# The last tile's third part in its own piece of PSUM, its first part's residual and store a tile earlier, and three stores right behind their residuals

## The chip, the cores and the metric

The kernel runs on one core of a Trainium2 chip. The metric is the device time of one execution in microseconds. The core's engines work side by side, each through its own queue in order: TensorE (PE in the profile; its weight loads are PEld), VectorE (DVE), ScalarE (ACT), GpSimd (POOL) and SyncE (SP), which here issues the transfers between the core and its memory. An engine waits for another one by semaphores.

## The reference

Two blocks stand one behind the other, on 2048 rows of 640 columns, in bfloat16:

```python
x = A_q
h = x + _A_ref(_layernorm(x, axis=-1), A_k, A_v, A_shift_k, A_ssm_k, A_ssm_D)
h2 = h + _B_ref(_layernorm(h, axis=-1), B_w1, B_b1, B_w2)
return h2
```

`_A_ref` is a short convolution of `k`, a product with `v`, a long convolution over all rows, and a product with the normalized input. The change doesn't touch it. `_B_ref` is a dense layer of two matrices with Mish in between:

```python
h = jnp.einsum("bsd,df->bsf", x, w1) + b1
sp = jnp.log1p(jnp.exp(-jnp.abs(h))) + jnp.where(h > 0, h, jnp.zeros_like(h))
act = h * jnp.tanh(sp)
return jnp.einsum("bsf,fd->bsd", act, w2)
```

The sum of `h` and the result of `_B_ref` is the output. The change lies in this sum and in the product with `w2` ahead of it.

## The kernel before

**Tiles.** The 2048 rows are 16 tiles of 128 rows. A tile's `h` lies in one of three buffers of the on-chip memory: `x0` (tiles 0 to 3; `x` in the profile), `xa` (4 to 9) and `xb` (10 to 15). For the dense layer the tiles are taken in five units of 2, 2, 4, 4 and 4 tiles. For a unit, the normalized rows are transposed: by TensorE for the first three units, and for tiles 8 to 15 by VectorE (`dtr8` and so on, line 788) and then by 16 small transfers for each pair of tiles (`d_tr8`, `d_tr10`, `d_tr12`, `d_tr14`, line 804). Then come seven steps `m1pe<unit>_<n>` of the first product (lines 845 and 849), each followed by Mish on ScalarE (`hb<unit>_<n>`, line 858).

**The second product.** For tile t, `m2pe<t>` is 28 matmuls (line 875): for each half of 320 columns, 14 matmuls of 128 rows by 320 columns, which add up in PSUM. When they are done, `res<t>` on VectorE (line 885) adds the PSUM result to the tile's rows in place, and `d_out<t>` on SP (line 890) stores the 160 KB.

**The last tile** is cut into three parts by columns, `TAIL`: 320, 224 and 96 of them. `m2ape15`, `m2bpe15` and `m2cpe15` are the matmuls of the three parts (14 each, line 875), `resa15`, `resb15` and `resc15` their residuals (line 882), `d_outa15`, `d_outb15` and `d_outc15` their stores (line 897). All three parts lie in one piece of PSUM. Part a takes columns 0 to 319 of the piece, part b columns 512 to 735 and part c columns 736 to 831.

**PSUM** is used as four pieces of 128 × 1024 float32 (`ps0` to `ps3`; `ps` in the profile), a ring named `R_PS`. A step that opens a result takes one, and the piece is free again when the last reader of that result is done. Where several are free, the planner takes the one that it expects to have come free first. The framework under the kernel sets the semaphores, from the order in which the instructions are written down and from the buffers that they touch.

**Order.** The order of all steps is written out by hand, as `ORDER`: a name and a letter for the engine (`t` TensorE, `a` ScalarE, `v` VectorE, `p` GpSimd, `d` the SP queue). On each engine the steps run in that order. `_schedule` gives each step a start by costs that the kernel holds, and the steps are written down in the order of these starts; so among engines it is these starts that decide which step is written down first. In the planner's times `resa15` starts when `res14` ends, which is after the start of `m2bpe15` and before that of `m2cpe15`.

In the order before, the last steps of TensorE are m2pe11, m1pe4_3, m2pe10, m2ape15, m2pe13, m2pe12, m2pe14, m2bpe15, m2cpe15; those of VectorE are res10, res13, res12, res14, resa15, resb15, resc15; and the stores on SP are d_out10, d_out13, d_out12, d_out14, d_out8, d_outb15, d_outa15, d_outc15. Earlier on SP, d_tr8 stands ahead of d_out1, d_out0 and d_tr10; d_out2 and d_out3 come behind d_tr10; d_out9 stands ahead of d_out4.

Of the kernel before, what the change touches and what calls it, by code (L numbers as in the profile page):

```python
# [27 lines left out]
TAIL = [(0, 320), (320, 224), (544, 96)]  # L28
# [31 lines left out]
hb0_2:a hb0_0:a m1pe0_1:t hb0_1:a m1pe0_3:t hb0_3:a wb6:v ln1_11:v trpe2:t pow3:p hc3:v m1pe0_5:t trev2:a hb0_5:a wb4:v wb5:v h5:p trpe3:t trev3:v  # L60
m1pe0_4:t h6:p ln1_14:v bn5:v wb7:v hb0_4:a ln1e3:p h4:v bn6:v bn4:v ln1p3:p m1pe1_2:t hb1_2:a pow5:p pow6:p m1pe1_3:t hb1_3:a lnx9:a pow4:p hc4:v
m1pe1_6:t hc6:v h7:v hc5:v m1pe1_1:t hb1_1:a m1pe1_0:t m1pe1_4:t hb1_6:a lnx8:a wb8:v h8:v lnx10:a hb1_0:a hb1_4:a m2pe1:t trpe4:t trpe6:t trev4:a
bn7:v pow7:p hc7:v trev6:a res1:v wb9:v h9:v bn9:v pow9:p m1pe1_5:t trpe5:t trpe7:t hb1_5:a bn8:v pow8:p hc8:v trev5:a hc9:v wb10:v dtr8:v dtr9:v
d_tr8:d d_out1:d m2pe0:t trev7:a m1pe2_6:t h10:p bn10:v pow10:p m1pe2_3:t hb2_3:a hb2_6:a res0:v d_out0:d hc10:v lnx11:a m1pe2_2:t ln1_12:v dtr10:v
ln1_15:v wb11:v ln1_13:v h11:v bn11:v pow11:p hb2_2:a hc11:v dtr11:v d_tr10:d ln1e4:v ln1p4:p lnx14:p m2pe2:t res2:v lnx13:p wb13:v i2pa14:t i2pb14:t
i2pa12:t i2pc14:t y14:a wb14:v i2pb12:t i2pc12:t y12:a m1pe2_1:t hb2_1:a m1pe2_5:t hb2_5:a i2pa15:t i2pb15:t i2pc15:t y15:v m1pe2_4:t hb2_4:a lnx15:a
d_out2:d h13:p lnx12:p wb12:p h12:p m1pe2_0:t m2pe3:t bn13:v pow13:p res3:v d_out3:d h14:v bn14:v pow14:p bn12:v pow12:p hc12:v dtr12:v hc13:v dtr13:v
hb2_0:a d_tr12:d m2pe5:t res5:v d_out5:d m2pe6:t res6:v d_out6:d m1pe3_2:t hb3_2:a wb15:v h15:p bn15:v pow15:p m2pe7:t res7:v d_out7:d hc14:v
m1pe3_1:t hb3_1:a m1pe3_0:t dtr14:v hb3_0:a hc15:v dtr15:v d_tr14:d m1pe3_4:t m1pe3_3:t hb3_3:a m1pe3_5:t hb3_5:a hb3_4:a m1pe3_6:t hb3_6:a m2pe4:t
res4:v m2pe9:t res9:v d_out9:d d_out4:d m2pe8:t res8:v m1pe4_1:t m1pe4_6:t hb4_6:a m1pe4_5:t hb4_5:a hb4_1:a m1pe4_4:t m1pe4_2:t hb4_2:a m1pe4_0:t  # L70
hb4_0:a m2pe11:t res11:v d_out11:d m1pe4_3:t hb4_3:a m2pe10:t res10:v d_out10:d hb4_4:a m2ape15:t m2pe13:t res13:v d_out13:d m2pe12:t res12:v
d_out12:d m2pe14:t res14:v d_out14:d resa15:v d_out8:d m2bpe15:t resb15:v d_outb15:d d_outa15:d m2cpe15:t resc15:v d_outc15:d
""".split()
UNITS = [256, 256, 512, 512, 512]

# [112 lines left out]
def _dve1(n):  # L188
    return 0.06 + 0.001045 * n
# [14 lines left out]
def _mm(n):  # L204
    return max(0.027, n / 2400.0 + 0.0025)
# [46 lines left out]
def kernel(  # L252
# [18 lines left out]
    def OP(name, opts, deps=(), allocs=(), uses=(), emit=None, prio=0.0, lat=0.0):  # L271
        o = _Op(name, opts if isinstance(opts, list) else [opts], deps, allocs, uses, emit, prio, lat)
        ops.append(o)
        return o
# [56 lines left out]
    for c in CHUNKS:  # L331
# [4 lines left out]
        for x in SWT[c.i]:  # L336
            t = blk(x)
# [16 lines left out]
    R_PS = _Ring(4)  # L354
# [12 lines left out]
    def ps_f32(rt):  # L367
        rt.tile = banks[rt.slot][:]
        return rt.tile
# [125 lines left out]
    for b in range(NDC):  # L495
        rt = _RT(R_PS)
# [17 lines left out]
    for m in range(NDC):  # L514
        for h in (1, 0):
            rt = _RT(R_PS)
# [13 lines left out]
            def kvf(e, m=m, h=h, rt=rt):  # L530
# [3 lines left out]
                             uses=[rt], emit=kvf, prio=9.2))  # L534
# [4 lines left out]
    for b in range(NDC):  # L539
        n = raw_n[b]  # L540
        rt = _RT(R_PS)
# [29 lines left out]
    for gi in range(22):  # L571
        rt = _RT(R_PS)
# [30 lines left out]
    for c in CHUNKS:  # L603
        nf = (32, 16, 8)[len(c.dcs) - 1]
        n = c.ng
        evs = []
        for gi in range(P // nf):
            rt = _RT(R_PS)
# [49 lines left out]
    for c in CHUNKS:  # L658
        for gi in range(c.ng // 8):
            rt = _RT(R_PS)  # L660
# [25 lines left out]
    w2_z = OP("w2z", ("pool", 1.25), k1_pes + d_adds, emit=emit_w2z, prio=7)  # L686
    d_w2 = DMA("d_w2", 2.2e6, emit_w2, deps=i1_pes[1] + d_w1, prio=7)
# [29 lines left out]
    for t2 in range(NT):  # L717
# [10 lines left out]
        rt = _RT(R_PS)  # L728
# [97 lines left out]
    def hb_of(u):  # L826
        return hb_s[u % 2]
# [4 lines left out]
    for u, w in enumerate(UNITS):  # L832
        t2s = list(range(c0 // P, (c0 + w) // P))
        hbs = []
        for fp in range(NFC // 2):
            rt = _RT(R_PS)

            def pe(e, u=u, fp=fp, rt=rt, w=w):
                ph = ps_f32(rt)
                for i in range(2):  # L840
                    fc = fp * 2 + i
                    if fc == NFC - 1:
                        for dc in range(NDC):
                            for o in (0, 64):
                                nc.tensor.matmul(ph[o:o + 64, 512:512 + w // 2], w1[:, dc, fc * P:FF], lnhT_of(u).rearrange("p t r c j -> p c (t r) j")[:, dc, o * w // 4096:(o + 64) * w // 4096],
                                                 start=(dc == 0), stop=(dc == NDC - 1))
                        continue
                    for dc in range(NDC):
                        nc.tensor.matmul(ph[:, i * 512:i * 512 + w], w1[:, dc, fc * P:fc * P + P], lnhT_of(u).rearrange("p t r c j -> p c (t r) j")[:, dc, 0:w // 32],  # L849
                                         start=(dc == 0), stop=(dc == NDC - 1))  # L850
            o_pe = OP(f"m1pe{u}_{fp}", ("pe", 10 * _mm(w) if fp < NFC // 2 - 1 else 7.5 * _mm(w) + 2 * _SWITCH), [tr_evs[t] for t in t2s] + d_w1 + mm2_last.get(u - 2, []), allocs=[rt],
                      uses=[lt_rts[u]], emit=pe, prio=100 + u)

            def hbf(e, u=u, fp=fp, rt=rt, w=w):
                for i in range(2):
                    fc = fp * 2 + i
                    n = w // 2 if fc == NFC - 1 else w
                    nc.scalar.activation(hb_of(u)[:, fc, 0:n], rt.tile[:, i * 512:i * 512 + n], ACT.Mish, bias=b1s[:, fc:fc + 1], scale=1.0)  # L858
            hbs.append(OP(f"hb{u}_{fp}", ("act", (2 if fp < NFC // 2 - 1 else 1.5) * _act(w) + 0.18), [o_pe, c_b1] + i1_pes[(1, 2)[u % 2]], uses=[rt], emit=hbf, prio=100 + u))
        lasts = []  # L860
        for tl, t2 in enumerate(t2s):
            rt = _RT(R_PS)

            def pe2(e, u=u, tl=tl, rt=rt, w=w, cols=((0, 320), (320, 320))):
                po = ps_f32(rt) if cols[0][0] == 0 else rt.tile
                for a, n in cols:
                    for fc in range(NFC):
                        o = tl * P
                        if w == P and fc == NFC - 1:
                            for h in range(2):  # L870
                                nc.tensor.matmul(po[64 * h:64 * h + 64, a + a // 320 * 192:a + a // 320 * 192 + n], hb_of(u)[:, fc, 0:64], w2[:, fc + h, a:a + n],
                                                 start=False, stop=True)
                            continue
                        x = 1 if fc == NFC - 1 and o >= w // 2 else 0
                        nc.tensor.matmul(po[:, a + a // 320 * 192:a + a // 320 * 192 + n], hb_of(u)[:, fc, o - x * w // 2:o - x * w // 2 + P], w2[:, fc + x, a:a + n],  # L875
                                         start=(fc == 0), stop=(fc == NFC - 1))

            def resf(e, t2=t2, rt=rt, part=None):
                if part:
                    a, n = part  # L880
                    x = xt(t2)[:, a:a + n]
                    nc.vector.tensor_tensor(x, rt.tile[:, a + a // 320 * 192:a + a // 320 * 192 + n], x, ALU.add)  # L882
                    return
                x = xt(t2).rearrange("p (a d) -> p a d", a=2)
                nc.vector.tensor_tensor(x, rt.tile[:].rearrange("p (a d) -> p a d", a=2)[:, :, 0:320], x, ALU.add)  # L885
            if t2 < NT - 1:
                o_pe2 = OP(f"m2pe{t2}", ("pe", 3.81), hbs + [d_w2, w2_z], allocs=[rt], emit=pe2, prio=100 + u + 0.5)
                lasts.append(o_pe2)
                o_res = OP(f"res{t2}", ("dve", _dve1(640)), [o_pe2], uses=[rt], emit=resf, prio=44)
                DMA(f"d_out{t2}", 164e3, (lambda t2=t2: nc.sync.dma_start(oview[:, t2, :], xt(t2))), deps=[o_res], prio=100 + u + 0.5)  # L890
                continue
            o_pe2 = None
            for i, (a, n) in enumerate(TAIL):
                o_pe2 = OP(f"m2{'abc'[i]}pe{t2}", ("pe", 14 * _mm(n) + 0.005), hbs + [d_w2, w2_z, o_pe2], allocs=[] if i else [rt], uses=[rt] if i else [], emit=(lambda e, f=pe2, a=a, n=n: f(e, cols=((a, n),))), prio=100 + u + 0.5)
                lasts.append(o_pe2)
                o_res = OP(f"res{'abc'[i]}{t2}", ("dve", _dve1(n)), [o_pe2], uses=[rt], emit=(lambda e, f=resf, a=a, n=n: f(e, part=(a, n))), prio=44)
                DMA(f"d_out{'abc'[i]}{t2}", n * 256, (lambda t2=t2, a=a, n=n: nc.sync.dma_start(oview[:, t2, a:a + n], xt(t2)[:, a:a + n])), deps=[o_res], prio=100 + u + 0.5)
        mm2_last[u] = lasts
        c0 += w
# [42 lines left out]
```

## Time and profile before

| | us |
|---|---|
| median of 3 runs | 232.42 (230.9 to 233.92) |
| the profiled execution, whole | 232.92 |
| its span, from the first to the last instruction | 231.1 |
| PE busy in the span | 218.8 (95%) |
| DVE, ACT, POOL busy | 141.7, 133.2, 63.8 |
| mean granted TensorE clock | 0.985 of full speed |

In a row of the timeline stand the start in the span, the length, the engine, the line of the kernel, the operation, what it writes and reads with the shapes, the number of instructions, and in brackets the idle time of the engine ahead of it with what ended that. `SPq` is SP's queue; the length of a transfer there is the time that issuing it took, not the transfer's own. In a row of the groups by form stand the shape and number, then the busy time and the mean length of one in ns, then idle time. In a row of the transfers stand what is written and read, the number, the size of one and the median time from issue to landing. In a row of the chain stand start, length and what held up the end; `issue` is time in which nothing visible was waited for. In a row of the stretches stand, for each engine, busy time and number of instructions, then the granted TensorE clock, the share of the transfer engines in use and GB/s. `q8 instruction` is the queue through which TensorE's instructions come in: packets, MB, share.

### The profile page before, as it was taken

The page shows a single profiled execution, that of the slowest core. Times are in us where ns is not written, and L with a number is a line of the kernel's source. Part 1 is how long each engine was busy: PE and PEld are TensorE (multiplying, and loading weights), DVE is VectorE, ACT ScalarE, POOL GpSimd, SP SyncE. Part 2 cuts the span into 40 slices and gives each one's busy share as a digit, 9 for nine tenths or more (in the row PEclk, how much of TensorE's full clock was granted, in tenths as well). Part 3 has the DMA queues.
Part 4 walks back from the last instruction along what each step waited for, and adds up shares of the span by engine and source line. Part 5 has one row for each costly group of instructions (what it writes and reads, how often), then busy time and mean ns, then how long its engine had stood idle before and what let it go on. Part 6 is the DMA issues. An engine that isn't in the chain of part 4 may idle for free.

```text
span 231.1 us, 6512 instructions
## 1 busy us (share of the span) xinstructions
PE 218.8 (95%) x2809; PEld 168.5 (73%) x2809; DVE 141.7 (61%) x262; ACT 133.2 (58%) x183; POOL 63.8 (28%) x87
## 2 busy tenths in 40 slices
PE   7996999999959999999999999999999999999991
PEld 2995999999859899889877474676545764567771
DVE  0786798889999698998968984477710120011121
ACT  2586799989997999699675264501137004512000
POOL 0517066006820028744921305922000000000000
PEclk9999799999997999999999999999999999999999
DMA  7999990693990059940000012120131010000002
GB/s 219 376 419 409 417 383 18 187 271 109 257 278 6 3 197 407 385 154 0 3 0 3 12 32 77 32 80 14 32 107 32 21 57 0 0 33 28 28 31 85
DMA packets 24479, 30.05 MB, mean 130 GB/s; under 512 B 6529, under 2 KB 20866, under 8 KB 24066
## 3 DMA queue, kind: packets, MB, share of 16 engines
q1 hardware_dynamic: 24160, 29.48, 36.9%
q8 instruction: 22, 0.36, 0.6%
q10 hardware_dynamic: 194, 0.15, 0.2%
q14 instruction: 7, 0.06, 0.1%
q0 software_dynamic: 96, 0.00, 0.0%
HBM read 20.45 MB, written 2.62 MB: 100 GB/s over the span
## 4 chain that ended last, share of the span: by engine, by line
PE 81%; ACT 5%; DVE 4%; issue 4%; DVEq 0%; ACTq 0%
PE ps L875 26%; PE ps L849 25%; PE ps L667 4%; PE ps L666 4%; ACT uv L377 4%; PE ps L737 4%; PE ps L579 4%; PE ps L472 3%; PE ps L615 3%; PE ps L502 2%; ACT uk L377 2%; DVE uk L379 2%; PE ps L525 1%; DVE uv L379 1%; PE ps L473 1%
## 5 line engine op out<-in xcount | busy, mean ns | idle before, releaser
L858 ACT ACTIVATE uv<-ps,b1s 128x512 bf16<-128x512 f32 (+1 forms) x70 | 36.4, 591 | 56.1 <-PE ps L849 36.2
L875 PE MATMUL ps<-rn,uv 128*128 128x320 bf16 (+2 forms) x462 | 62.4, 295 | 0.6 <-DVE xb L882 0.6
L849 PE MATMUL ps<-G 128*128 128x512 bf16 (+1 forms) x325 | 58.8, 337 | 0.2 <-DVE G L379 0.2
L875 PEld LDWEIGHTS <-uv 128*128 128x128 bf16 x462 | 44.4, 98 | 18.1 <-issue 0.9
L377 ACT CAST uk<-ps 128x1024 bf16<-128x1024 f32 (+2 forms) x52 | 47.5, 1032 | 5.7 <-PE ps L473 3.5
L849 PEld LDWEIGHTS <-G 128*128 128x128 bf16 x325 | 31.2, 98 | 23.5 <-issue 0.7
L377 ACT CAST uv<-ps 128x1024 bf16<-128x1024 f32 x32 | 29.8, 1084 | 1.7 <-PE ps L615 1.7
L885 DVE TENSOR_TENSOR xb<-ps,xb 128x640 bf16<-128x640 f32 x5 | 4.1, 825 | 31.5 <-PE ps L875 31.5
L666 PE MATMUL ps<-a,uv 128*128 128x128 bf16 x160 | 19.6, 227 | 0.3 <-ACT uv L377 0.3
L666 PEld LDWEIGHTS <-uv 128*128 128x128 bf16 x160 | 18.4, 116 | 0.0
L885 DVE TENSOR_TENSOR xa<-ps,xa 128x640 bf16<-128x640 f32 x6 | 4.8, 814 | 20.4 <-PE ps L875 20.4
L768 POOL TENSOR_TENSOR r<-ve,mhalf 128x1 f32<-128x1 f32 x16 | 8.9, 561 | 24.1 <-DVE ve L765 24.1
L615 PE MATMUL ps<-uv,G 128*128 128x64 bf16 (+1 forms) x384 | 12.6, 189 | 2.7 <-issue 2.4
L379 DVE CAST uk<-ps 128x1024 bf16<-128x1024 f32 (+1 forms) x10 | 12.1, 1217 | 4.8 <-PE ps L473 2.7
L615 PEld LDWEIGHTS <-G 128*128 128x128 bf16 x384 | 11.9, 98 | 3.1 <-issue 2.8
L531 DVE TENSOR_TENSOR ra<-ps,rb 128x1024 bf16<-128x1024 f32 x10 | 12.1, 1222 | 1.4 <-PE ps L526 1.3
L579 PE MATMUL ps<-uk,G 128*128 128x160 bf16 x128 | 11.6, 231 | 0.1
L631 DVE TENSOR_TENSOR uv<-uv,uk 128x1024 bf16<-128x1024 bf16 x18 | 11.4, 684 | 0.1
L472 PE MATMUL ps<-cst,ra 128*64 128x128 bf16 x160 | 10.2, 219 | 0.5 <-ACT uv L377 0.5
L737 PE MATMUL ps<-uk,ra 128*128 128x128 bf16 (+1 forms) x128 | 10.2, 232 | 0.3 <-ACT uk L377 0.2
L473 PE MATMUL ps<-cst,ra 128*64 128x128 bf16 x160 | 10.3, 221 | 0.0
L379 DVE CAST uv<-ps 128x1024 bf16<-128x1024 f32 x8 | 9.5, 1219 | 1.1 <-PE ps L473 0.7
(114 smaller groups left out, 366.8 us busy)
## 6 DMA issues: line engine op xcount, KB each, us to landing
G<-tab_g SPq DMA_DIRECT2D x8, 512.0 KB, 12.1
rn<-in_A_ssm_k_dram SPq DMA_DIRECT2D x5, 512.0 KB, 6.1
ra<-in_A_k_dram SPq DMA_DIRECT2D x4, 640.0 KB, 10.4
rb<-in_A_v_dram SPq DMA_DIRECT2D x2, 1280.0 KB, 14.1
G<-in_B_w_dram SPq DMA_DIRECT2D x5, 432.0 KB, 7.9
rn<-in_B_w_dram SPq DMA_DIRECT2D x1, 2080.0 KB, 15.5
rn<-uk SPq DMA_DIRECT2D x4, 512.0 KB, 4.7
rb<-uk SPq DMA_DIRECT2D x4, 512.0 KB, 6.5
```

What stands on the lines that cost most here:

```text
L377: nc.scalar.copy(o, i)
L379: nc.vector.tensor_copy(o, i)
L472: nc.tensor.matmul(ps[0:64, dgl, :], lhs, mc, start=True, stop=True)
L473: nc.tensor.matmul(ps[64:128, dgl, :], lhs, ms, start=True, stop=True)
L531: nc.vector.tensor_tensor(kv_w[:, m, :, 8 * h:8 * h + 8, :], rt.tile.rearrange("p (l t d) -> p d t l", l=4, t=8), raw_v[:, 8 * h:8 * h + 8 ...
L579: nc.tensor.matmul(ps[:, o:o + 160], g_v[:, f, :], KA[:, :, f, :], start=True, stop=True)
L615: nc.tensor.matmul(ps[:, fl * st:fl * st + n], g_v[:, f0 + fl, :], V[c.i][:, :, f0 + fl, :], start=True, stop=True)
L666: nc.tensor.matmul(pz[:, dgl, :], V[c.i][:, dg // 4, :, dg % 4], a12[:, 0, :], start=True, stop=False)
L737: nc.tensor.matmul(py[:, o:o + w], t2m[:, t2, ri, :], Z[c.i][:, ri * NT + t2, o - c.c0:o - c.c0 + w], start=(ri == 0), stop=(ri == 1))
L849: nc.tensor.matmul(ph[:, i * 512:i * 512 + w], w1[:, dc, fc * P:fc * P + P], lnhT_of(u).rearrange("p t r c j -> p c (t r) j")[:, dc, 0:w / ...
L858: nc.scalar.activation(hb_of(u)[:, fc, 0:n], rt.tile[:, i * 512:i * 512 + n], ACT.Mish, bias=b1s[:, fc:fc + 1], scale=1.0)
L875: nc.tensor.matmul(po[:, a + a // 320 * 192:a + a // 320 * 192 + n], hb_of(u)[:, fc, o - x * w // 2:o - x * w // 2 + P], w2[:, fc + x, a:a ...
```

## The change

Three things are edited, two of them in the written order.

1. `m2cpe15`, the last tile's third part, opens a piece of PSUM of its own, which `resc15` reads. The first and second part share one as before.
2. `resa15` moves from behind `res14` to behind `res12` on VectorE, and `d_outa15` from behind `d_outb15` to ahead of `d_out14` on SP. So TensorE's order is as before, VectorE's is res12, resa15, res14, resb15, resc15, and SP's is d_out12, d_outa15, d_out14, d_outb15, d_outc15.
3. Stores move up to right behind their residuals: `d_out1` ahead of `d_tr8`; `d_out2` behind `res2` (no other transfer lies between its old and its new place); `d_out4` ahead of `d_out9`; and `d_out8` from behind `d_out14` to behind `res8`, ahead of `d_out11`.

Nothing of the computation changes. The diff, cut to the lines of the order that differ in more than the line break, and the code:

```diff
-bn7:v pow7:p hc7:v trev6:a res1:v wb9:v h9:v bn9:v pow9:p m1pe1_5:t trpe5:t trpe7:t hb1_5:a bn8:v pow8:p hc8:v trev5:a hc9:v wb10:v dtr8:v dtr9:v
-d_tr8:d d_out1:d m2pe0:t trev7:a m1pe2_6:t h10:p bn10:v pow10:p m1pe2_3:t hb2_3:a hb2_6:a res0:v d_out0:d hc10:v lnx11:a m1pe2_2:t ln1_12:v dtr10:v
+bn7:v pow7:p hc7:v trev6:a res1:v d_out1:d wb9:v h9:v bn9:v pow9:p m1pe1_5:t trpe5:t trpe7:t hb1_5:a bn8:v pow8:p hc8:v trev5:a hc9:v wb10:v dtr8:v
+dtr9:v d_tr8:d m2pe0:t trev7:a m1pe2_6:t h10:p bn10:v pow10:p m1pe2_3:t hb2_3:a hb2_6:a res0:v d_out0:d hc10:v lnx11:a m1pe2_2:t ln1_12:v dtr10:v
...
-res4:v m2pe9:t res9:v d_out9:d d_out4:d m2pe8:t res8:v m1pe4_1:t m1pe4_6:t hb4_6:a m1pe4_5:t hb4_5:a hb4_1:a m1pe4_4:t m1pe4_2:t hb4_2:a m1pe4_0:t
-hb4_0:a m2pe11:t res11:v d_out11:d m1pe4_3:t hb4_3:a m2pe10:t res10:v d_out10:d hb4_4:a m2ape15:t m2pe13:t res13:v d_out13:d m2pe12:t res12:v
-d_out12:d m2pe14:t res14:v d_out14:d resa15:v d_out8:d m2bpe15:t resb15:v d_outb15:d d_outa15:d m2cpe15:t resc15:v d_outc15:d
+res4:v d_out4:d m2pe9:t res9:v d_out9:d m2pe8:t res8:v d_out8:d m1pe4_1:t m1pe4_6:t hb4_6:a m1pe4_5:t hb4_5:a hb4_1:a m1pe4_4:t m1pe4_2:t hb4_2:a
+m1pe4_0:t hb4_0:a m2pe11:t res11:v d_out11:d m1pe4_3:t hb4_3:a m2pe10:t res10:v d_out10:d hb4_4:a m2ape15:t m2pe13:t res13:v d_out13:d m2pe12:t
+res12:v d_out12:d resa15:v d_outa15:d m2pe14:t res14:v d_out14:d m2bpe15:t resb15:v d_outb15:d m2cpe15:t resc15:v d_outc15:d
...
-                po = ps_f32(rt) if cols[0][0] == 0 else rt.tile
+                po = ps_f32(rt) if cols[0][0] in (0, TAIL[-1][0]) else rt.tile
...
             for i, (a, n) in enumerate(TAIL):
-                o_pe2 = OP(f"m2{'abc'[i]}pe{t2}", ("pe", 14 * _mm(n) + 0.005), hbs + [d_w2, w2_z, o_pe2], allocs=[] if i else [rt], uses=[rt] if i else [], emit=(lambda e, f=pe2, a=a, n=n: f(e, cols=((a, n),))), prio=100 + u + 0.5)
+                if i == len(TAIL) - 1:
+                    rt = _RT(R_PS)
+                o_pe2 = OP(f"m2{'abc'[i]}pe{t2}", ("pe", 14 * _mm(n) + 0.005), hbs + [d_w2, w2_z, o_pe2], allocs=[] if i == 1 else [rt], uses=[rt] if i == 1 else [], emit=(lambda e, f=pe2, a=a, n=n, rt=rt: f(e, rt=rt, cols=((a, n),))), prio=100 + u + 0.5)
                 lasts.append(o_pe2)
-                o_res = OP(f"res{'abc'[i]}{t2}", ("dve", _dve1(n)), [o_pe2], uses=[rt], emit=(lambda e, f=resf, a=a, n=n: f(e, part=(a, n))), prio=44)
+                o_res = OP(f"res{'abc'[i]}{t2}", ("dve", _dve1(n)), [o_pe2], uses=[rt], emit=(lambda e, f=resf, a=a, n=n, rt=rt: f(e, rt=rt, part=(a, n))), prio=44)
```

More of the change, by code (lines that the diff above doesn't have):

```diff
@@ L62 @@
 m1pe1_6:t hc6:v h7:v hc5:v m1pe1_1:t hb1_1:a m1pe1_0:t m1pe1_4:t hb1_6:a lnx8:a wb8:v h8:v lnx10:a hb1_0:a hb1_4:a m2pe1:t trpe4:t trpe6:t trev4:a
-bn7:v pow7:p hc7:v trev6:a res1:v wb9:v h9:v bn9:v pow9:p m1pe1_5:t trpe5:t trpe7:t hb1_5:a bn8:v pow8:p hc8:v trev5:a hc9:v wb10:v dtr8:v dtr9:v
-d_tr8:d d_out1:d m2pe0:t trev7:a m1pe2_6:t h10:p bn10:v pow10:p m1pe2_3:t hb2_3:a hb2_6:a res0:v d_out0:d hc10:v lnx11:a m1pe2_2:t ln1_12:v dtr10:v
-ln1_15:v wb11:v ln1_13:v h11:v bn11:v pow11:p hb2_2:a hc11:v dtr11:v d_tr10:d ln1e4:v ln1p4:p lnx14:p m2pe2:t res2:v lnx13:p wb13:v i2pa14:t i2pb14:t
@@ L66 @@
-i2pa12:t i2pc14:t y14:a wb14:v i2pb12:t i2pc12:t y12:a m1pe2_1:t hb2_1:a m1pe2_5:t hb2_5:a i2pa15:t i2pb15:t i2pc15:t y15:v m1pe2_4:t hb2_4:a lnx15:a
-d_out2:d h13:p lnx12:p wb12:p h12:p m1pe2_0:t m2pe3:t bn13:v pow13:p res3:v d_out3:d h14:v bn14:v pow14:p bn12:v pow12:p hc12:v dtr12:v hc13:v dtr13:v
+bn7:v pow7:p hc7:v trev6:a res1:v d_out1:d wb9:v h9:v bn9:v pow9:p m1pe1_5:t trpe5:t trpe7:t hb1_5:a bn8:v pow8:p hc8:v trev5:a hc9:v wb10:v dtr8:v
+dtr9:v d_tr8:d m2pe0:t trev7:a m1pe2_6:t h10:p bn10:v pow10:p m1pe2_3:t hb2_3:a hb2_6:a res0:v d_out0:d hc10:v lnx11:a m1pe2_2:t ln1_12:v dtr10:v
@@ L68 @@
+ln1_15:v wb11:v ln1_13:v h11:v bn11:v pow11:p hb2_2:a hc11:v dtr11:v d_tr10:d ln1e4:v ln1p4:p lnx14:p m2pe2:t res2:v d_out2:d lnx13:p wb13:v i2pa14:t
+i2pb14:t i2pa12:t i2pc14:t y14:a wb14:v i2pb12:t i2pc12:t y12:a m1pe2_1:t hb2_1:a m1pe2_5:t hb2_5:a i2pa15:t i2pb15:t i2pc15:t y15:v m1pe2_4:t hb2_4:a
+lnx15:a h13:p lnx12:p wb12:p h12:p m1pe2_0:t m2pe3:t bn13:v pow13:p res3:v d_out3:d h14:v bn14:v pow14:p bn12:v pow12:p hc12:v dtr12:v hc13:v dtr13:v
 hb2_0:a d_tr12:d m2pe5:t res5:v d_out5:d m2pe6:t res6:v d_out6:d m1pe3_2:t hb3_2:a wb15:v h15:p bn15:v pow15:p m2pe7:t res7:v d_out7:d hc14:v
```

## The prediction

> **What bounds the kernel now.** I read the page first: the span is 231.1 us, and the profiled execution took 232.92 us, 1.8 more than its span. Then the chain of waits from 110 us on, for this change edits nothing that runs earlier.
>
> ```profile
> span 231.1 us, 6512 instructions
> ```
>
> ```profile
> by line: PE ps L875 50.2%; PE ps L849 41.1%; PE ps L845 2.0%; PE ps L737 1.4%; PE ps L816 0.9%; DVE xb L882 0.7%; DVEq L937 0.1%; issue 0.1%
> 109.95 3.38 PE ps L849 x31
> ...
> 207.23 18.47 PE ps L875 x140
> 225.70 0.02 issue
> 225.72 0.50 DVE xb L882
> ...
> 226.27 0.77 PE ps L875 x14
> ...
> 227.06 0.39 DVE xb L882
> 227.45 0.17 DVEq L937
> ```
>
> Its columns are start, length and what held the end. From 109.95 to 225.70 us every piece is PE work and each begins where the last one ended: no store, residual or transfer in that stretch holds anything. Only at 225.70, when m2bpe15 (the second part of the last tile) is done, do other engines come onto the chain. So the change can gain only behind 225.70, a stretch of 231.1 − 225.70 = 5.4 us, and can lose ahead of it only by opening a gap in PE's work.
>
> The same stretch by instruction, with the idle time ahead of each and what ended it, and then the SP queue's stores one by one:
>
> ```profile
> 220.65 0.82 DVE L885 TENSOR_TENSOR xb<-ps,xb 128x640 bf16<-128x640 f32 x1 [2.98 <-PE ps L875]
> 224.38 0.82 DVE L885 TENSOR_TENSOR xb<-ps,xb 128x640 bf16<-128x640 f32 x1 [2.91 <-PE ps L875]
> 225.72 0.49 DVE L882 TENSOR_TENSOR xb<-ps,xb 128x320 bf16<-128x320 f32 x1 [0.52 <-PE ps L875]
> 226.27 0.76 PE L875 MATMUL ps<-rn,uv 128*128 128x96 bf16 x14 [0.58 <-DVE xb L882]
> 227.06 0.56 DVE L882 TENSOR_TENSOR xb<-ps,xb 128x224 bf16<-128x224 f32 x2 [0.85 <-PE ps L875]
> ```
>
> ```profile
> 225.23 0.33 SPq L890 DMA_DIRECT2D out_dram<-xb  x1
> 227.52 0.33 SPq L897 DMA_DIRECT2D out_dram<-xb  x1
> 227.90 0.90 SPq L897 DMA_DIRECT2D out_dram<-xb  x2
> 228.42 0.38 SPq L897 DMA_DIRECT2D out_dram<-xb  x1
> ```
>
> Four things are to be seen. resa15 (320 columns) starts at 225.72, just as m2bpe15 ends, although its own matmuls, m2ape15, came before those of tiles 13, 12 and 14, which the 140 matmuls of the chain hold too, and VectorE had been idle 0.52 us: a wait on the shared piece of PSUM, not on data. m2cpe15 then stands 0.58 us until resa15 has read that piece. resb15, whose data were there at 225.70, starts at 227.06, behind m2cpe15. And resc15 is done at 227.06 + 0.56 = 227.62, but its store, d_outc15, is issued at 228.42 behind d_outb15 (227.52) and d_outa15 (227.90). From that issue to the end of the span are 231.1 − 228.42 = 2.68 us.
>
> **The change part by part.** The durations of its pieces:
>
> ```profile
> L875 PEld LDWEIGHTS <-uv 128*128 128x128 bf16 x29 | 2.1, 98 | 0.9 <-issue 0.7
> L875 PE MATMUL ps<-rn,uv 128*128 128x224 bf16 x14 | 1.5, 259 | 0.0
> L875 PE MATMUL ps<-rn,uv 128*128 128x96 bf16 x14 | 0.8, 206 | 0.6 <-DVE xb L882 0.6
> L882 DVE TENSOR_TENSOR xb<-ps,xb 128x320 bf16<-128x320 f32 x1 | 0.5, 492 | 0.5 <-PE ps L875 0.5
> L882 DVE TENSOR_TENSOR xb<-ps,xb 128x224 bf16<-128x224 f32 x1 | 0.4, 391 | 0.8 <-PE ps L875 0.8
> L882 DVE TENSOR_TENSOR xb<-ps,xb 128x96 bf16<-128x96 f32 x1 | 0.2, 247 | 0.0
> ```
>
> *resa15 and d_outa15 a tile ahead.* In the written order resa15 now stands behind res12, ahead of m2bpe15. res12 ends at 220.65 + 0.82 = 221.47; resa15 takes 0.49, to about 222.0. It lies in the 2.91 us in which VectorE waited for tile 14, so it costs nothing; without that cover it would cost its 0.49. Its new duty, that m2bpe15 must not write the piece before resa15 has read it, is met 2 us early, since m2bpe15 begins after tile 14's matmuls, whose residual starts at 224.38. Its store goes out at about 222.1, between those of tiles 12 and 14, on a queue that is empty there (the next issue is at 225.23).
>
> *The third part in its own piece.* There are four pieces. The planner gives m2cpe15 the one that came free first, and that is tile 13's, whose residual was over before 220.65. So neither resa15 nor resb15 stands ahead of m2cpe15, and m2cpe15 no longer stands ahead of resb15. Worked out: 14 matmuls of 96 columns take 0.76 us, of which 0.206 is one record, so they start (0.76 − 0.206) / 13 = 0.043 us apart; those of 224 columns start (1.5 − 0.259) / 13 = 0.095 apart. The last of m2bpe15 starts at 225.70 − 0.26 = 225.44, the first of m2cpe15 at 225.54, the last 13 × 0.043 = 0.56 later, and it ends at 226.30. Were nothing of it to overlap with m2bpe15, it would end at 225.70 + 0.77 = 226.47; that is the other bound.
>
> The Trainium skill ("TensorE: Matmul & The Clock Gate", Back-to-back issue gap) gives a stream of weight load and matmul pairs about 81 ns per matmul at 128 columns, and it speaks against so short a third part. As an estimate by that page, m2cpe15 would end near 226.80 and the gain would be about 0.5 us smaller. The row above has these very 14 pairs at 43 ns, so the row is used.
>
> *VectorE and the stores at the end.* resb15 runs 225.72 to 226.11, beside m2cpe15; d_outb15 follows 0.07 later (227.06 + 0.39 = 227.45 against 227.52), at 226.18. resc15 runs 226.32 to 226.57, and its store could go at 226.64. SP is free for it: stores of this kind were issued 0.38 (227.52 to 227.90) and 0.52 apart (227.90 to 228.42), so from 226.56 or 226.70 on. d_outc15 moves from 228.42 to 226.64, 1.78 us earlier, or to 226.81, 1.61 earlier, by the other bound. I take 1.7. It is made of the wait on resa15 and the overlap of the third part (227.04 to 226.30), resb15 no longer in front of resc15 (about 0.3), and the two stores no longer in front of the last (about 0.7).
>
> What else could end last then? Landings by size:
>
> ```profile
> out_dram<-xb SPq DMA_DIRECT2D x5, 160.0 KB, 1.8
> out_dram<-xb SPq DMA_DIRECT2D x1, 80.0 KB, 1.7
> out_dram<-xb SPq DMA_DIRECT2D x1, 56.0 KB, 1.6
> out_dram<-xb SPq DMA_DIRECT2D x1, 24.0 KB, 1.5
> ```
>
> Tile 14's store lands at 225.23 + 1.8 = 227.0, d_outb15 at 227.8, d_outc15 at 226.64 + 1.5 = 228.1: still the last, with the same 2.68 us from its issue to the end.
>
> *Stores behind their residuals.* Each passes others on the SP queue.
>
> ```profile
> 121.67 0.82 DVE L885 TENSOR_TENSOR x<-ps,x 128x640 bf16<-128x640 f32 x1
> 129.80 10.32 SPq L804 DMA_DIRECT2D G<-uv  x16
> 140.16 2.46 SPq L890 DMA_DIRECT2D out_dram<-x  x2
> 142.74 10.59 SPq L804 DMA_DIRECT2D G<-uv  x16
> 158.44 2.32 PE L849 MATMUL ps<-G 128*128 128x512 bf16 x10
> 181.12 0.82 DVE L885 TENSOR_TENSOR xa<-ps,xa 128x640 bf16<-128x640 f32 x1 [12.93 <-PE ps L875]
> 185.78 0.81 SPq L890 DMA_DIRECT2D out_dram<-xa  x2
> ```
>
> d_out1 moves ahead of the 16 transfers of d_tr8. Its residual ends at 122.49, 7 us before d_tr8 can start, so d_tr8 doesn't wait for it; d_out0 and d_tr10 behind it move up by a part of the 2.46 us that the two stores took. The work that needs d_tr10 starts at 158.44 in a gapless PE, so that is worth nothing; nor would a delay of a few us cost anything, for d_tr10's last issue ended at 153.33. d_out4 goes out at about 182.0 in place of behind d_out9 near 186; nobody waits for either. d_out2 passes no other transfer. d_out8, which stands last ahead of tile 15's stores now, goes out right behind its residual, far ahead of the end; nobody waits for it. I take zero for all of these. From both sides: a gain is excluded, because PE decides up to 225.70; the loss is bounded below, as the last rival.
>
> **The rivals.**
>
> *The third part is not freed, or is slower.* If m2cpe15 still waited for resb15 (the change not doing what it says), it would start at 226.11 + 0.06 = 226.17 and end at 226.94, and d_outc15 would go at 227.28: 1.14 us gained. If the 98 ns weight loads set its pace, it would end at 225.54 + 13 × 0.098 + 0.206 = 227.02, and 1.06 would be gained. For the first: such a wait stands in this trace, twice. Against it: the allocation in the diff, and three other pieces free by then. For the second nothing but the length of that row; against it, the matmuls' own row at 43 ns. Time: about 231.3. The pace of 81 ns that the Trainium skill gives in the section named above lies between those two rows.
>
> *The last store is held.* Of the two stores at 140.16 the second took 1.74 us to issue, 1.36 more than the 0.38 of d_outc15 in this trace.
>
> ```profile
> 140.89 1.74 SPq L890 DMA_DIRECT2D out_dram<-x  x1
> ```
>
> If d_outc15, 0.46 behind d_outb15, met that, 0.3 us would be left of the gain: 232.1. Against it: that store came straight behind 16 transfers and another store, and the three stores from 227.52 on took 0.38 to 0.52 each in a row.
>
> *Slower: PE waits for its code.* PE's instructions come in blocks over the same DMA engines. One block is loaded in each of the stretches 122 to 124 and 182 to 184 us, exactly where d_out1 and d_out4 now go.
>
> ```profile
> q8 instruction: 1, 0.02, 4.5%
> ```
>
> ```profile
> q8 instruction: 1, 0.02, 4.2%
> ```
>
> If PE had no reserve of instructions, each store would delay its block by up to its landing, 1.8 us in the rows above: 3.6 lost against 1.7 gained, 234.3. With landings of twice that it would be 7.2, and 237.9. It decides from the point at which a late block costs PE more than 0.85 us each. Against it: the same meeting is in this trace already. Between 140 and 143 us a block came in beside both stores, and PE was busy 3.00 of 3.00 us:
>
> ```profile
> q8 instruction: 1, 0.02, 3.0%
> ```
>
> ```profile
> 140.00:143.00 3.00, 3.00 (x21) 1.67 (x20) 1.06 (x3) 1.84 (x3) 2.31 (x5) 1.00 0.25 73
> ```
>
> The Trainium skill ("Runtime: NRT & Kernel Launch", Instruction fetch mechanics) says that the next block is fetched while the current one executes and that crossing a block is mostly hidden; the gapless chain agrees.
>
> **How the numbers follow.** 232.92 − 1.7 = 231.2 us for the profiled execution. That one lies 0.5 above the median of the three runs, 232.42, so the forecast for a median is 232.42 − 1.7 = 230.7 us, 0.7% less. Chances: 0.72 for it; 0.10 for a third part not freed or slow (231.3); 0.09 for a gain lost at the last store (232.1); 0.09 for a gap in PE (from 232.5 up to 238). The three runs lie 1.5 us to either side of their median. So the range goes from 229.0 (the larger gain, and scatter downward) to 232.9, which holds the first three cases and the mild end of the fourth. Two per cent, about what a measurement of this kernel can tell from no change, is 4.6 us, nearly the whole stretch behind 225.70. Of that stretch at least a residual and the 2.68 us remain, so a gain over 2% is 0.03, for scatter alone. A loss over 2% needs the fourth case well beyond its mild end: 0.05. The rest is 0.92.
>
> **What would show it.** In the profile of the changed kernel: the 96-column matmuls directly behind the 224-column ones with no idle time ahead of them; the 320-column residual near 221.5 us of today's clock, in front of tile 14's; the 224-column one at the end of m2bpe15; only two stores behind tile 14's; and 2.7 us from the last issue to the end. PE's chain up to m2bpe15 should still be without a gap. The forecast is wrong if that chain shows an idle time of 0.5 us or more, if the 96-column matmuls wait for VectorE, or if the last store is issued over 1.2 us after m2bpe15's end.

## The result, and the profile after

The median fell from 232.59 to 230.74 us (21 runs of each). The medians lie 1.85 us apart. The ratio of the runs is 0.9925, with a 95% interval of 0.9903 to 0.9948, which is 1.7 us less (1.2 to 2.3). The forecast was 1.7.

The chain of waits of the changed kernel from 110 us on (start, length, what held the end):

```profile
114.19 0.40 PE ps L845 x10
...
208.08 19.07 PE ps L875 x154
227.15 0.03 issue
227.17 0.26 DVE xb L882
```

Where the chain of before ran through TensorE, resa15, m2cpe15 and resb15, it now runs through TensorE to the very end of the third part (154 matmuls in one piece, 14 more than before) and then through one residual. By instruction, VectorE's and SP's part of it:

```profile
span 230.1 us, 6516 instructions
```

```profile
221.50 0.82 DVE L885 TENSOR_TENSOR xb<-ps,xb 128x640 bf16<-128x640 f32 x1 [2.98 <-PE ps L875]
222.24 0.48 DVE L882 TENSOR_TENSOR xb<-ps,xb 128x320 bf16<-128x320 f32 x1
225.23 0.82 DVE L885 TENSOR_TENSOR xb<-ps,xb 128x640 bf16<-128x640 f32 x1 [2.51 <-PE ps L875]
226.57 0.39 DVE L882 TENSOR_TENSOR xb<-ps,xb 128x224 bf16<-128x224 f32 x1 [0.52 <-PE ps L875]
226.99 0.33 SPq L899 DMA_DIRECT2D out_dram<-xb  x1
227.17 0.26 DVE L882 TENSOR_TENSOR xb<-ps,xb 128x96 bf16<-128x96 f32 x1 [0.20 <-PE ps L875]
227.45 0.34 SPq L899 DMA_DIRECT2D out_dram<-xb  x1
```

(The change adds two lines ahead of line 897, so the stores of the last tile stand at line 899 here.) resa15 runs behind res12. resb15 starts when m2bpe15 ends, resc15 when m2cpe15 ends, and the last store goes out at 227.45, 0.02 us after resc15's end (227.17 + 0.26). It also goes out 0.46 us behind d_outb15, and the stores before were issued 0.38 and 0.52 apart: the residual and the SP queue let the last store go at about the same time.

The span fell by only 231.1 − 230.1 = 1.0 us, less than the median, and that is a trap: the profiled execution of the changed kernel took 231.87 us, the most of its 21 runs. TensorE's chain, gapless in both from 110 us on, stands 0.85 us later in this one execution: its steps of line 845 are at 114.19, in before at

```profile
113.34 0.40 PE ps L845 x10
```

The edits begin behind that point. So each profile below is read from a fixed mark near the end: the start of tile 14's residual, to the end of the span. That is 231.1 − 224.38 = 6.72 us before and 230.1 − 225.23 = 4.87 us changed, 1.85 less. Spans are printed to 0.1 us, so such a stretch is good to about 0.05 us. From 80 us on the granted clock is 1.00 in all nine profiles, so their ends can be compared. m2bpe15 ends 1.32 us behind the mark (225.70 − 224.38). The profile of the first part moved up alone comes from a slow execution of that kernel, which is why its span doesn't fit its ratio.

### The profile page after: what moved, and what is told of

It is laid out like the page before. It is cut to its first block, busy times and chain, and to the rows that moved or that the text cites. A ratio compares the mean times of both kernels' runs of the same rounds, so it can differ in the third digit from the quotient of the medians.

```text
span 230.1 us, 6516 instructions
## 1 busy us (share of the span) xinstructions
PE 219.2 (95%) x2809; PEld 168.9 (73%) x2809; DVE 141.5 (62%) x262; ACT 133.3 (58%) x183; POOL 63.8 (28%) x87
## 4 chain that ended last, share of the span: by engine, by line
PE 82%; ACT 6%; issue 4%; DVE 4%; DMA 3%; SPq 0%; DVEq 0%; ACTq 0%
PE ps L875 27%; PE ps L849 25%; ACT uv L377 4%; PE ps L667 4%; PE ps L579 4%; PE ps L666 4%; PE ps L737 4%; PE ps L615 3%; PE ps L472 3%; DMA rn<-in_A_ssm_k_dram 3%; PE ps L502 2%; ACT uk L377 2%; PE ps L546 2%; DVE uk L379 2%; PE ps L525 1%
```

## The experiments

The first three kernels ran 8, 12 and 12 times beside the kernel before. The last four ran once each (231.76, 230.43, 229.59 and 229.96 us), so they are read by their traces alone.

**The third part's piece alone.** The code of the change (the diff is cut to its main lines) with the written order of before.

```diff
+                if i == len(TAIL) - 1:
+                    rt = _RT(R_PS)
```

> Only the third part's own piece of PSUM; the written order is that of before. The measure is the stretch from the end of m2bpe15 to the end of the span: 5.4 us before, 3.6 us in the changed kernel. Theory A (three waits add up: resa15 held by the shared piece, the third part and resb15 holding each other, and the three stores in a row on SP): m2cpe15 follows m2bpe15 directly, but resa15 still starts only when m2bpe15 ends, resb15 stands behind it (about 0.9 us after m2bpe15's end it is done), and d_outb15, d_outa15, d_outc15 go out one behind the other; d_outc15 about 1.8 us after m2bpe15's end, against 2.7 before and 0.9 changed. Stretch 4.5 us, ratio about 0.996. Theory B (the piece of PSUM is all of the gain): stretch 3.6 us, ratio 0.9925. Theory C (the stores moved upstream are the gain): 5.4 us, ratio 1.000.

Measured: ratio 0.9927 (0.9895 to 0.9959), which doesn't decide between theories A and B: B's 0.9925 lies in its middle, A's 0.996 at its upper end. The trace does:

```profile
span 228.6 us, 6512 instructions
```

```profile
222.83 0.82 DVE L885 TENSOR_TENSOR xb<-ps,xb 128x640 bf16<-128x640 f32 x1 [2.91 <-PE ps L875]
224.07 0.42 SPq L890 DMA_DIRECT2D out_dram<-xa  x1
224.17 0.95 DVE L882 TENSOR_TENSOR xb<-ps,xb 128x320 bf16<-128x320 f32 x3 [0.52 <-PE ps L875]
225.03 1.29 SPq L899 DMA_DIRECT2D out_dram<-xb  x3
```

resa15 still starts 1.34 us behind the mark, when m2bpe15 ends; the three residuals follow each other in 0.95 us, and the three stores take 1.29. From the mark to the end 228.6 − 222.83 = 5.77 us, from m2bpe15's end 4.45: theory A's 4.5.

**The first part moved up alone.** The code of before; only the order is edited.

```diff
-d_out12:d m2pe14:t res14:v d_out14:d resa15:v d_out8:d m2bpe15:t resb15:v d_outb15:d d_outa15:d m2cpe15:t resc15:v d_outc15:d
+d_out12:d resa15:v d_outa15:d m2pe14:t res14:v d_out14:d d_out8:d m2bpe15:t resb15:v d_outb15:d m2cpe15:t resc15:v d_outc15:d
```

> Only resa15 and d_outa15 moved up; all three parts in one piece as before. Theory A: resa15 is written down ahead of m2bpe15 and m2cpe15, so neither waits for it later, and m2cpe15 follows m2bpe15 directly although it shares the piece; what is left is that resb15 waits for m2cpe15 (0.6 us after m2bpe15's end), then resc15. d_outb15 about 1.1 and d_outc15 about 1.5 us after m2bpe15's end. Stretch 4.1 to 4.2 us, ratio about 0.9945. Theory B (the piece is all): the third part still waits and the stretch stays at 5.4 us, ratio 1.000. Theory C: 5.4 us, ratio 1.000.

Measured: ratio 0.9932 (0.9897 to 0.9968).

```profile
span 231.2 us, 6513 instructions
```

```profile
208.54 19.07 PE ps L875 x154
227.61 0.02 issue
227.63 0.39 DVE xb L882
```

```profile
225.69 0.82 DVE L885 TENSOR_TENSOR xb<-ps,xb 128x640 bf16<-128x640 f32 x1 [2.51 <-PE ps L875]
227.63 0.55 DVE L882 TENSOR_TENSOR xb<-ps,xb 128x224 bf16<-128x224 f32 x2 [1.11 <-PE ps L875]
```

TensorE runs 154 matmuls without a gap, although the third part shares the piece: its wait for resa15 is gone because resa15 is early, not because of the piece. What sharing still costs is resb15, which starts at 227.63, with the end of m2cpe15, and not 0.6 us sooner. From the mark 231.2 − 225.69 = 5.51 us, from m2bpe15's end 4.19, as theory A has it. Theory B falls.

**The four stores alone.** The code of before; d_out1, d_out2, d_out4 and d_out8 right behind res1, res2, res4 and res8. The diff is cut to the places where d_out1, d_out4 and d_out8 are put in.

```diff
-bn7:v pow7:p hc7:v trev6:a res1:v wb9:v h9:v
+bn7:v pow7:p hc7:v trev6:a res1:v d_out1:d wb9:v h9:v
...
-res4:v m2pe9:t res9:v d_out9:d d_out4:d m2pe8:t res8:v
+res4:v d_out4:d m2pe9:t res9:v d_out9:d m2pe8:t res8:v d_out8:d
```

> Only d_out1, d_out2, d_out4 and d_out8 moved to behind their residuals. Theory A: PE's chain stays without a gap and the end of the kernel is as before: stretch 5.4 us, ratio 1.000, within 0.2%. Theory C (these stores, or d_out8 gone from in front of the last three, are a part of the gain): ratio 0.9925 to 0.997. The last rival of the prediction (code blocks of TensorE late beside d_out1 and d_out4): a gap in PE of 0.85 us or more near 123 or 183 us, ratio above 1.003.

Measured: ratio 1.0008 (0.9974 to 1.0042). Its chain at the end has the same pieces as that of before:

```profile
207.86 18.47 PE ps L875 x140
226.33 0.02 issue
226.36 0.50 DVE xb L882
226.86 0.04 issue
226.90 0.77 PE ps L875 x14
227.67 0.02 issue
227.69 0.39 DVE xb L882
```

The span is 231.8 us, so 231.8 − 226.33 = 5.5 us from m2bpe15's end, as before within the rounding of the spans. TensorE was busy for all of the 108 us from 115 to 223. The runs leave room for 0.3% of gain or 0.4% of loss; the trace shows nothing of either from these four moves. Theory C falls, and so does the rival of late code blocks as far as these stores go.

**Three pieces, order of before.** Each part opens a piece; resa15 stands behind res14, d_outa15 behind d_outb15. The diff is against the code of the change, and of its long line only the two edited pieces are shown.

```diff
-                if i == len(TAIL) - 1:
+                if i:
                     rt = _RT(R_PS)
...
-allocs=[] if i == 1 else [rt], uses=[rt] if i == 1 else []
+allocs=[rt], uses=[]
```

> Each part of the last tile in a piece of PSUM of its own; written order of before, so resa15 still stands behind res14 and d_outa15 behind d_outb15. Theory A (resa15 waited for the shared piece, not for data): resa15 starts right behind res14, about 0.45 us before m2bpe15's end, m2bpe15 and m2cpe15 follow without a gap, resb15 starts at m2bpe15's end; only the row of three stores is left, d_outc15 about 1.4 us after m2bpe15's end. Stretch about 4.1 us. If resa15 waited for something else than the piece, it starts again at m2bpe15's end and d_outc15 goes 1.8 us after it: 4.5 us.

```profile
span 230.0 us, 6512 instructions
```

```profile
224.57 0.82 DVE L885 TENSOR_TENSOR xb<-ps,xb 128x640 bf16<-128x640 f32 x1 [2.91 <-PE ps L875]
225.32 0.99 DVE L882 TENSOR_TENSOR xb<-ps,xb 128x320 bf16<-128x320 f32 x2
226.37 1.33 SPq L899 DMA_DIRECT2D out_dram<-xb  x3
226.51 0.26 DVE L882 TENSOR_TENSOR xb<-ps,xb 128x96 bf16<-128x96 f32 x1 [0.20 <-PE ps L875]
```

resa15 now starts at 225.32, straight behind res14 and with no idle time, in the very place in the order where it stood idle 0.52 us before. So it was the shared piece, and nothing else, that held it. The end comes 230.0 − 224.57 = 5.43 us behind the mark, or 4.11 behind m2bpe15's end. The row of three stores (1.33 us) is what is left.

**The first part's store late again.** The changed kernel with one step put back in the order of SP.

```diff
-res12:v d_out12:d resa15:v d_outa15:d m2pe14:t res14:v d_out14:d m2bpe15:t resb15:v d_outb15:d m2cpe15:t resc15:v d_outc15:d
+res12:v d_out12:d resa15:v m2pe14:t res14:v d_out14:d m2bpe15:t resb15:v d_outb15:d d_outa15:d m2cpe15:t resc15:v d_outc15:d
```

> The changed kernel with one thing put back: d_outa15 stands behind d_outb15 on SP again (resa15 stays early, the third part keeps its piece). Theory A (three stores in a row hold the last one by their issue): d_outb15 goes out about 0.45 us after the end of m2bpe15 as in the changed kernel, d_outa15 0.4 behind it, d_outc15 0.4 to 0.5 behind that, at 1.3 to 1.4 us in place of 0.9. From the start of tile 14's residual to the end of the span: 5.3 to 5.4 us, against 4.9 changed and 6.8 before. If SP's row of stores costs nothing (the last store waits for resc15 alone): 4.9 us.

```profile
223.28 0.82 DVE L885 TENSOR_TENSOR xb<-ps,xb 128x640 bf16<-128x640 f32 x1 [2.51 <-PE ps L875]
225.08 0.33 SPq L899 DMA_DIRECT2D out_dram<-xb  x1
225.22 0.26 DVE L882 TENSOR_TENSOR xb<-ps,xb 128x96 bf16<-128x96 f32 x1 [0.20 <-PE ps L875]
225.47 0.42 SPq L899 DMA_DIRECT2D out_dram<-xb  x1
225.98 0.38 SPq L899 DMA_DIRECT2D out_dram<-xb  x1
```

resc15 is done at 225.22 + 0.26 = 225.48, when d_outa15 has just been begun, and the last store follows that one at 225.98, 0.50 us after its data were ready. The span is 228.6 us: 5.32 from the mark against 4.87. So the place of that one store, whose data had been ready for over 4 us, is worth about 0.45 us.

**Parts of 320, 256 and 64 columns** in the changed kernel.

```diff
-TAIL = [(0, 320), (320, 224), (544, 96)]
+TAIL = [(0, 320), (320, 256), (576, 64)]
```

> The changed kernel with parts of 320, 256 and 64 columns in place of 320, 224 and 96. Two questions. First, what paces the third part: by columns, the 64-column matmuls start 0.028 us apart (0.43 ns per column, as those of 96 and 224 do); by the weight loads, 0.043 us or more. Second, what bounds the end now: theory A says that with the shorter third part the issue of d_outb15 on SP (0.4 to 0.5 us) ends behind resc15 and sets the start of d_outc15, so the end comes no earlier, but 0.1 to 0.2 us later, since m2bpe15 is 0.19 us longer: 5.0 to 5.1 us from the start of tile 14's residual to the end of the span, against 4.9. If the third part's matmuls and residual alone decide, it is 4.8 to 4.9 us.

```profile
span 227.8 us, 6516 instructions
```

```profile
222.75 0.82 DVE L885 TENSOR_TENSOR xb<-ps,xb 128x640 bf16<-128x640 f32 x1 [2.51 <-PE ps L875]
224.27 0.63 DVE L882 TENSOR_TENSOR xb<-ps,xb 128x256 bf16<-128x256 f32 x2 [0.70 <-PE ps L875]
224.72 0.81 SPq L899 DMA_DIRECT2D out_dram<-xb  x2
225.15 0.38 SPq L899 DMA_DIRECT2D out_dram<-xb  x1
```

```profile
L875 PE MATMUL ps<-rn,uv 128*128 128x64 bf16 x14 | 0.6, 193 | 0.0
```

Two answers. The matmuls of 64 columns start about (0.6 − 0.193) / 13 = 0.031 us apart, where those of 96 took 0.043: the pace goes with the columns. The weight loads don't set it, for 14 of them at 98 ns one behind another would take 1.4 us. The Trainium skill ("TensorE: Matmul & The Clock Gate", Back-to-back issue gap) has about 81 ns per pair at 128 columns; these runs don't bear that out. In the chain of before, ten pairs of that very width on line 816 take 56 ns each:

```profile
120.92 0.56 PE ps L816 x10
```

The second answer: the end comes 227.8 − 222.75 = 5.05 us behind the mark, 0.18 later than with 96 columns: both residuals are done at 224.27 + 0.63 = 224.90, but the last store goes at 225.15, 0.43 behind the one before it. So this shorter third part gains nothing: the SP queue now holds the last store. (Its one timed run, 229.59 us, lies inside the scatter of the changed kernel's runs, 228.78 to 231.87, and says nothing against that.)

**Transfers at full load.** The changed kernel with 16 loads of 640 KB added behind d_out4, into buffers that are no longer read; nothing of the output depends on them. The diff is cut to the loads themselves.

```diff
+        for dst, src in ((uk[:, 0:10240], k), (uk[:, 10240:20480], v), (ra, k), (rb, v)):
+            for i in range(4):
+                nc.sync.dma_start(dst[:, i * 2560:(i + 1) * 2560], src[:, i * 2560:(i + 1) * 2560])
```

> The changed kernel with 16 loads of 640 KB added behind d_out4 (10.5 MB into buffers that nobody reads any more), so that the transfer engines are full from about 183 to 209 us, across one or two of the blocks in which TensorE's instructions come. Theory A (a block comes long before PE needs it, so the moved stores couldn't hurt): PE's chain stays without a gap, and the stretch from tile 14's residual to the end stays at 4.9 us; only the stores in between land later. The last rival of the prediction (a block beside transfers comes late): a gap in PE of 0.85 us or more between 183 and 215 us, the end later by as much, and the moved stores were safe only by their small size.

The transfers between 203 and 207 us, TensorE's work in that stretch (busy time and number, then weight loads, VectorE, ScalarE, GpSimd, granted clock, share of the transfer engines, GB/s), and the mark:

```profile
q8 instruction: 1, 0.02, 1.7%
```

```profile
203.00:207.00 4.00, 4.00 (x26) 2.29 (x25) 0.82 (x1) 0.78 (x2) 0.00 (x0) 1.00 1.03 414
```

```profile
199.37 1.93 SPq L890 DMA_DIRECT2D out_dram<-xa  x2
223.33 0.82 DVE L885 TENSOR_TENSOR xb<-ps,xb 128x640 bf16<-128x640 f32 x1 [2.51 <-PE ps L875]
```

A block of TensorE's code came in while the transfer engines moved 414 GB/s, and TensorE was busy 4.00 of 4.00 us; its chain has no gap up to the end of m2cpe15. The two stores behind the loads went out at 199.37, where the changed kernel issues them within 8 us of 182.83, and nothing waited for them. The span is 228.2 us, so 4.87 from the mark, as without the loads. So that block was not late even beside far more traffic than the moved stores make. How much more it would take is not shown.

## Why the prediction was right

**That only the 5.4 us behind m2bpe15 could gain.** Right: the four upstream stores alone gave 1.0008, and TensorE's chain has no gap up to m2bpe15's end in any of these kernels.

**The new times at the end.** The prediction had d_outc15 0.94 us behind m2bpe15's end (226.64 − 225.70); it went 227.45 − 226.55 = 0.90 behind it, with m2bpe15's end from the mark. The 2.68 us from the last issue to the end of the span were 230.1 − 227.45 = 2.65. From 2.72 us (228.42 − 225.70) to 0.90 are 1.82 us, a little past the upper of the two bounds (1.61 and 1.78). The third part overlaps with the second as worked out from the matmuls' spacing: it ends 227.15 − 226.55 = 0.60 us behind it, the forecast's 226.30 − 225.70. The rest is the last store, 0.02 and not 0.07 us behind resc15.

**The median of 230.7.** That it came to 230.74 is in part luck. The gain was nearer 1.85 than 1.7, and the forecast started from 232.42, the median of three runs, where 21 runs of the kernel before gave 232.59. The two errors, of 0.15 and 0.17 us, cancel.

**Which edit does what.** Here the prediction was too simple. It let the third part's own piece remove its wait for resa15. The run with the first part moved up alone shows that the earlier place does this by itself. What the changed kernel gains beyond that is 5.51 − 4.87 = 0.64 us at the end, mainly by the own piece: resb15 no longer stands behind m2cpe15. (The changed kernel also has the four stores moved, which were worth nothing alone; no run has the first two edits without them.) The two edits overlap: each alone gives 0.95 (6.72 − 5.77) and 1.21 us (6.72 − 5.51), together 1.85 and not 2.16. The sum was right because it was made as a new schedule of the end, not as a sum over edits.

**Two stores no longer ahead of the last, about 0.7.** In the old schedule the last store waited 228.42 − 227.62 = 0.80 us for the queue. Put back into the new one, d_outa15 costs about 0.45, since only its own issue then lies in the way; d_outb15, which still goes out ahead of the last store, is issued while m2cpe15 and resc15 run.

**Zero for the stores behind their residuals.** Right, and the run at full load shows that there was room to spare. d_tr10 did move up, from 142.74 to

```profile
141.73 11.18 SPq L804 DMA_DIRECT2D G<-uv  x16
```

in an execution that is itself 0.85 us later, and it was worth nothing.

**The rivals.** A third part not freed, or paced by weight loads: not seen (14 matmuls without idle time ahead of them, and the pace of the 64-column run). A last store held 1.4 us: not seen, it was issued in 0.34 us. Code blocks late: not seen with the four stores alone, and not at full load either.

## What to carry to other kernels

When one engine is gapless up to a point, only the stretch behind that point can gain: write out its schedule anew, engine by engine, each queue included, instead of adding up the edits. Look for waits on a buffer in which the reader's own data have long been there; an earlier place in the written order or a buffer of its own each remove them, and they overlap. To judge a gain below the scatter of the runs, measure in the trace from a fixed mark near the end, for the span mixes in what happened far upstream.

## What was not expected

How far the start of the gapless stretch wanders. The same step of line 845, which all of these kernels reach by the same work, lies at 111.63 in one profile (parts of 320, 256 and 64 columns) and at 114.12 in another (the changed kernel):

```profile
111.63 0.47 PE L845 MATMUL ps<-G 128*64 128x128 bf16 x10
```

```profile
114.12 0.47 PE L845 MATMUL ps<-G 128*64 128x128 bf16 x10
```

These 2.5 us are most of what the runs of one kernel scatter (228.78 to 231.87 for the changed one), and they arise ahead of everything that was edited. A part of them goes with TensorE's clock. Between 20 and 30 us, with the transfer engines full in both, it was granted 1.00 in the first of the two and 0.83 in the second (the number behind the busy times):

```profile
20.00:30.00 10.00, 8.26 (x152) 7.84 (x150) 8.20 (x12) 8.10 (x11) 3.30 (x3) 1.00 1.03 418
20.00:30.00 10.00, 7.72 (x131) 7.21 (x131) 6.40 (x8) 6.41 (x8) 2.04 (x1) 0.83 1.03 413
```

The runs of the changed kernel fall into groups by their mean granted clock, too: at 0.985 eight runs took 231.08 to 231.87 us, at 0.993 eleven took 229.63 to 230.85, and at 1.000 two took 228.78 and 229.84. What makes the clock drop was not tried. Of the nine profiles the four with 0.83 there have this step between 113.27 and 114.58, and four of the five with 1.00 between 111.63 and 112.22. The fifth, that of the three pieces, has it at 113.46, so the clock there is not all of it.

The wait for the shared piece was not one that the data needed. Parts a and b lie in columns 0 to 319 and 512 to 735 of it, 4 bytes each. The Trainium skill ("PSUM — Partial Sum Buffer", The four PSUM rules) has banks of 512 float32, each its own memory, so these two lie in different banks. Yet in the kernel before, resa15 waited 0.52 us for m2bpe15, and with pieces of their own it didn't. That fits a framework that orders all accesses to a piece, whichever columns they touch; the semaphores themselves were not looked at.
